# Attention, mixture of experts and feed-forward on one core: shifted low words of the w_in conversion in PSUM, row maxima finished on transposed rows

## The chip, the cores and the metric

The kernel runs on one core of one Trainium2 chip. The metric is the device time in microseconds, the median of several runs. The engines are PE (TensorE, matrix products and transposes), DVE (VectorE), ACT (ScalarE), POOL (GpSimd) and SP (SyncE, which issues the DMAs). Each works through its own queue in order. On chip there are SBUF, and PSUM, into which PE writes and which DVE and ACT can read and write.

## The reference

Three stages follow one another: an attention in which a query sees only keys of its own hash bucket, a soft mixture of eight experts, and h - tanh(h) between two products.

```python
q_bits = (np.einsum('bhsd,dk->bhsk', q, proj) > 0)         # 6 bits; the same for k
mask = q_bucket[:, :, :, None] == k_bucket[:, :, None, :]
scores = np.where(mask, scale * (q @ k.T), -1e9)            # 2 x 8 heads, 768 x 768, 64 wide
scores = scores - np.max(scores, axis=-1, keepdims=True)
attn = np.exp(scores); attn = attn / (attn.sum(-1, keepdims=True) + 1e-09)
x = attn @ v                                                # as 1536 x 512
...
logits = x @ phi                                            # soft experts: softmax over tokens,
slot_input = d.T @ x                                        # over slots, relu(. @ w1[e]) @ w2[e]
...
h = x @ w_in                                                # 512 x 2048, float64
return (h - np.tanh(h)) @ w_out                             # 2048 x 512, float64
```

The weights w_in and w_out arrive as float64. The kernel takes them as pairs of 32-bit words and makes float32 of them with shifts and masks.

## The kernel before, in words

Attention works on eight pairs of heads, numbered i = 0 to 7. For a pair and a chunk of 128 rows there are these pieces of work, each a function that the order strings call by a short name:

- `m` (m_unit, L441): PE makes a 128x768 tile of scores from the leading parts (L446), DVE takes the maximum of each row (L447) into one column of `mx`, 128x12 when the pair is done.
- `f1` (m_fin1, L449): from `mx` DVE makes on 128x12 elements the flag of a row that has no key in its bucket (L454) and its offset (L455), both in `col`.
- `f2` (m_fin2, L458): PE transposes `col` into a PSUM tile `pc` (L462), ACT copies it to `row` (L464), and SP sends the 24 rows of 128 to where they are used: the offsets into row 96 of the operand QA, the flags four times into `z`.
- `s0`, `s1` (s_unit, L500): scores of one head with keys as rows (L504, L506), exponential on ACT (L508), running sum over the keys on POOL (L513, L519). `a` (av_unit, L522): product with v (L531). `xr`, `xe`, `x2`, `x3`, `lg`: row sums (L542), their transposes `prt` (L562) and reciprocals `rs` (L564, L567), tokens by features (px, L587, and xtok, L591), logits (L601, L604).
- `t0`, `t1`, `b`, `h0` to `h3`, `l0` to `l3`, `d`, `kc`, `v1`, `v2`: transposes of q and k (L353), bucket bits (L362, L365), leading parts on ACT (L406), remainders on DVE (L429 to L436), copies, and sums of v (L481 to L497).
- `wl`, `wc` (win_load, win_cvt): w_in comes in 16 parts of 128x512. For each, ACT rescales the high word into `cg` (L174), and DVE runs three instructions: the low word shifted into `cl` (L178), `cg` shifted and joined to it (L187), and the sign bit from the raw high word joined to that, into `win` (L192). `cl` is an SBUF tile of its own.

The order is written out by hand and is the order of every engine's queue:

```python
STEP = ("s0 l1 d s1 a lp m xe s0 m xr e00 v m s1 m s0 l0 m lp m a m s1 l2 v1 m a m m m l3 a wl lp "
        "wc t1 s0 t0 s1 s0 m e01 f1 h0 lp a lp h1 x2 lp wl f2 e02 s1 h3 lp v2 b e03 x3 wc wl s0 s1 "
        "h2 kc a lp wl wc lg qk").split()
```

STEP runs once for each pair i = 0 to 6 ("STEP 2" is the one with i = 2); START goes ahead of it with the first pair's maxima, and LAST serves pair 7. Beside the scores of pair i it finishes the maxima of pair i + 1 and prepares pair i + 2. START converts two of the parts of w_in, STEP 0 to 3 three each, STEP 4 two; STEP 5 and 6 find none left. STEP 5 also holds the first half's weights over its tokens (`e00` to `e03`). `lp` loads pieces of the expert weights, from STEP 5 on, as places come free.

PSUM in attention is a ring of three tiles of 128x768, handed out in turn by `psum()`, and two tiles for the product with v (`pav`). Who asks for the next tile gets the one given out three requests before, and waits until that one's readers are done.

After attention come the experts (the order string MOE) and the feed-forward stage (RUN and a loop), where the words of w_out are converted with the same helper functions in SBUF, and L1184 to L1190 compute h - tanh(h): L1189 reads two SBUF tiles, L1190 an SBUF tile and the PSUM tile `ph`.

Of the kernel before, what the change touches and what calls it, by code (L numbers as in the profile page):

```python
# [10 lines left out]
F32 = mybir.dt.float32  # L11
# [21 lines left out]
# columns of the constant table  # L33
# [8 lines left out]
# from here on, parts that are not on chip all the time  # L42
# [5 lines left out]
# h - tanh(h) = C h z ((z + A)^2 + B), z = h^2, below SMALL  # L48
# [13 lines left out]
# order of the work: before the first pair of heads, for one pair of heads, beside which the next three are prepared, and for  # L62
# the last pair
START = ("const.0 warm.3 qk.0 const.1 tq_aaaa.0 wl.0 oi.0 tk_aavv.0 h1.0 h0.0 bq.0 wl.0 bk.0 h2.0 "
        "h3.0 wq1p.0 m.0 m.0 m.0 l0.0 m.0 const.2 m.0 v.0 wk1a.0 m.0 m.0 m.0 wq0p.0 m.0 kc.0 m.0 "
        "m.0 qk.1 l2.0 m.0 wl.0 d.0 f1.0 wc.0 wk0s.0 t0.1 f2.0 h1.1 t1.1 l1.0 h3.1 l3.0 v1.0 h2.1 "
        "kc.1 oi.1 b.1 v2.0 wc.0 wc.0 h0.1 qk.2 oi.2 wl.0").split()
STEP = ("s0 l1 d s1 a lp m xe s0 m xr e00 v m s1 m s0 l0 m lp m a m s1 l2 v1 m a m m m l3 a wl lp "
        "wc t1 s0 t0 s1 s0 m e01 f1 h0 lp a lp h1 x2 lp wl f2 e02 s1 h3 lp v2 b e03 x3 wc wl s0 s1 "
# [3 lines left out]
# the experts, and the start of the last product with its first chunks  # L73
# [12 lines left out]
def constants():  # L86
# [5 lines left out]
    for pr in range(3):  # L92
        # rows (e2, n2, slot): the slots of expert 2 pr + e2
        ok = ((r % 32)[:, None] == np.arange(32)[None, :]) & (((r % 32) // SPE) == 2 * pr + r // 64)[:, None]
        c[:, C_SELPR + 32 * pr:C_SELPR + 32 * pr + 32] = ok
    for e2 in range(2):
        # rows (n4, slot): the slots of one of the last two experts
        o = C_SELE + 32 * e2
        c[:, o:o + 32] = c[:, C_SEL4:C_SEL4 + 32] * (np.arange(32) // SPE == 6 + e2)
    # mask rows out of bits b: q side [b, 1 - b], k side [-M (1 - b), -M b], for both heads  # L100
    for g in range(4):
        for h in range(2):
            for j in range(2 * NB):
# [7 lines left out]
                if g in (0, 2):  # L111
                    # the first pair of heads: both heads' bits on the q side, the head's own on the k side
                    o = C_FIRST + 2 * (g // 2 + g // 2 * h)
                    c[2 * D // 2 + 2 * NB * h + j, o:o + 2] = m, a
# [11 lines left out]
def body(ctx: ExitStack, tc: tile.TileContext, q, k, v, proj, phi, w1, w2, w_in, w_out, cst, out, dbg=None):  # L126
# [18 lines left out]
    # tokens by features, one half of the batch after the other  # L145
# [24 lines left out]
    # ------------------------------------------------------------------ float64 words to float32  # L170
    # raw [P, n, 2] words (low, high); the exponent is rebased on the high word read as float32
# [27 lines left out]
    # ------------------------------------------------------------------ weights of the experts, in pieces of 8 KB  # L199
    # a piece is half of one expert's w1 (two chunks of 128 rows) or w2 (512 rows, or 256 columns for the last two)  # L200
# [5 lines left out]
    # then places for w_out in halves, and its float64 words, 256 rows at a time  # L206
# [13 lines left out]
    # the first HOLD places take one piece each, and then tiles that stay  # L220
# [28 lines left out]
    # ------------------------------------------------------------------ attention  # L249
    def attention():  # L250
# [6 lines left out]
        # what is done with first comes last  # L257
# [21 lines left out]
        # operands: score products are [kh; mask, 1].[qh; mask, -m] + [kh; kl].[ql; qh]  # L279
        last = NPR - 1  # L280
        # both heads in one tile, but for the places of the last pair
# [21 lines left out]
        mx, cols, zr, vz, es, pav, xtu, rsT, rinv, uses = {}, {}, {}, {}, {}, {}, {}, {}, {}, {}  # L303
# [4 lines left out]
        # the last pair takes places of its weights  # L308
# [22 lines left out]
        # transposes of q or k: rows (head, d), columns (c, p)  # L331
        def t_unit(i, which, engs="aaaa"):
# [3 lines left out]
            if i == 0:  # L336
                # came as (h c d) and not as (c h d): rows (c odd or even, d), columns (half c, p)
# [19 lines left out]
        # bucket bits of q and k, as rows of the mask products  # L357
# [17 lines left out]
        # for the first pair where they go  # L375
# [22 lines left out]
        # leading parts  # L398
# [25 lines left out]
        # remainders, where each of the two inputs sits in the same partitions  # L424
# [14 lines left out]
        # row maxima over the keys, from the leading parts  # L439
# [9 lines left out]
        def m_fin1(i, hs=(0, 1)):  # L449
            n = len(hs)  # L450
            m = mx[i][:, hs[0] * KT:(hs[-1] + 1) * KT]
            col = pre.tile([P, 2 * n, KT], F32, tag="col", name="col")
            zc = col[:, 0:n, :].rearrange("p r c -> p (r c)")
            nc.vector.tensor_scalar(zc, m, -0.5 * MASK, None, ALU.is_lt)  # L454
            nc.vector.scalar_tensor_tensor(col[:, n:2 * n, :].rearrange("p r c -> p (r c)"), zc, -FAR, m, ALU.mult, ALU.subtract)  # L455
            cols[i] = col

        def m_fin2(i, hs=(0, 1)):  # L458
            s, n = i % 3, len(hs)
            col = cols.pop(i)  # L460
            pc = psum("pc")
            nc.tensor.transpose(pc[:2 * n * KT, :P], col.rearrange("p r c -> p (r c)"), ident)  # L462
            row = pre.tile([2 * n * KT, P], F32R, tag="row", name="row")
            nc.scalar.activation(row, pc[:2 * n * KT, :P], AF.Copy)  # L464
            if i not in zr:
                zr[i] = lap.tile([4, KT, P], F32R, tag="z", name="z")
            if QA2[s] is None:
                for j, h in enumerate(hs):
                    copy(QA[s][h][96:97].rearrange("o (c j) -> o c j", c=KT), row[(n + j) * KT:(n + j + 1) * KT, :])
            else:  # L470
                copy(QA2[s][96:97, hs[0]:hs[-1] + 1].rearrange("o h (c j) -> o (h c) j", c=KT), row[n * KT:, :])
            for r in range(4):
                if r % 2 in hs:
                    j = r % 2 - hs[0]
                    copy(zr[i][r:r + 1], row[KT * j:KT * j + KT, :])

        # sums of v over the keys, for rows whose bucket holds no key
# [56 lines left out]
        # row sums, in token layout after x2  # L534
# [35 lines left out]
        # both uses of the sums  # L570
# [24 lines left out]
        # logits of the slots, one head beside the other before the row sums are divided out  # L595
# [18 lines left out]
        # w_in to float32, a part at a time  # L614
# [13 lines left out]
        def win_cvt():  # L628
            if raws:
                raw, c, fq = raws.pop(0)  # L630
                g = cv.tile([P, 512], F32, tag="cg", name="cg")
                l = cv.tile([P, 512], U32, tag="cl", name="cl", bufs=1)
                cvt_b(cvt_a(raw, g, l), win[:, c, fq * 512:(fq + 1) * 512])

        # weights of batch 0 over its tokens, while the other batch goes through attention
        d0 = {}

        def disp0(n):
# [14 lines left out]
            "f1": m_fin1, "f2": m_fin2, "v": load_v, "v1": v_unit, "v2": v_unit2, "qk": load_qk,  # L653
# [7 lines left out]
        for h in range(2):  # L661
            units[f"f1{h}"] = lambda i, h=h: m_fin1(i, (h,))
            units[f"f2{h}"] = lambda i, h=h: m_fin2(i, (h,))
# [49 lines left out]
        # while nothing has arrived yet  # L713
# [57 lines left out]
    # products nobody reads, while the tensor engine would wait and its clock would drop  # L771
# [4 lines left out]
    # weights over the tokens, one half of the batch at a time and with the maxima so far  # L776
# [9 lines left out]
    # the share of the first half has its own maxima  # L786
# [12 lines left out]
    # sums of tokens under those weights, and of the weights: rows (part of the tokens, slot)  # L799
# [20 lines left out]
    # ------------------------------------------------------------------ soft mixture of experts  # L820
# [528 lines left out]
```

## Time and profile before

| | us |
|---|---|
| runs of the kernel before | 533.79, 535.04, 538.79; median 535.04 |
| span of the profiled execution (one execution of its own; the page gives no time beside its span) | 533.6 |
| PE busy, matrix products | 474.6 |
| DVE busy | 388.8 |
| POOL busy | 302.2 |
| ACT busy | 273.3 |

The span is cut in 40 slices in the profile's second part; a digit is the busy share of a slice in tenths, PEclk the clock that was granted to TensorE:

```text
PE   7879787997997879989899899997888888999996
DVE  5959699897998989855814338539999998655552
POOL 4887758676677678757855310006666656444442
PEclk9689799898999999979989999999999999999999
```

The other views are: windows (busy time of each engine in a stretch of the span), groups of instructions by line and shape, one line's instructions with their minimum, median and maximum, timelines of one engine (start, length, and in brackets the idle time before with what ended it), and the chain: the work that ended last, followed back from the end of the span, each step to what released it.

### The profile page before, as it was taken

The page shows a single profiled execution, that of the slowest core. Times are in us where ns is not written, and L with a number is a line of the kernel's source. Part 1 is how long each engine was busy: PE and PEld are TensorE (multiplying, and loading weights), DVE is VectorE, ACT ScalarE, POOL GpSimd, SP SyncE. Part 2 cuts the span into 40 slices and gives each one's busy share as a digit, 9 for nine tenths or more (in the row PEclk, how much of TensorE's full clock was granted, in tenths as well). Part 3 has the DMA queues.
Part 4 walks back from the last instruction along what each step waited for, and adds up shares of the span by engine and source line. Part 5 has one row for each costly group of instructions (what it writes and reads, how often), then busy time and mean ns, then how long its engine had stood idle before and what let it go on. Part 6 is the DMA issues. An engine that isn't in the chain of part 4 may idle for free.

```text
span 533.6 us, 7452 instructions
## 1 busy us (share of the span) xinstructions
PE 474.6 (89%) x2634; PEld 304.8 (57%) x2634; DVE 388.8 (73%) x493; ACT 273.3 (51%) x471; POOL 302.2 (57%) x243
## 2 busy tenths in 40 slices
PE   7879787997997879989899899997888888999996
PEld 3445444555555446555466544365666566888884
DVE  5959699897998989855814338539999998655552
ACT  6344644726546346345244211138767775766662
POOL 4887758676677678757855310006666656444442
PEclk9689799898999999979989999999999999999999
DMA  6445183281631813927538699998000000300003
GB/s 210 107 109 145 48 179 109 65 189 41 143 111 48 202 47 69 327 101 206 220 126 316 266 336 401 364 392 332 1 0 1 1 0 0 119 1 2 1 1 123
DMA packets 51572, 72.83 MB, mean 136 GB/s; under 512 B 25604, under 2 KB 33480, under 8 KB 51528
## 3 DMA queue, kind: packets, MB, share of 16 engines
q1 hardware_dynamic: 51528, 72.28, 42.9%
q8 instruction: 23, 0.38, 0.3%
q14 instruction: 21, 0.17, 0.1%
HBM read 60.08 MB, written 3.15 MB: 118 GB/s over the span
## 4 chain that ended last, share of the span: by engine, by line
DVE 47%; PE 43%; issue 3%; POOL 3%; ACT 2%; DMA 1%; DVEq 0%; SPq 0%; ACTq 0%; POOLq 0%
DVE mx L447 9%; DVE win L192 7%; DVE win L1189 5%; PE pav L531 5%; PE po L1240 5%; PE po L1239 5%; PE po L1241 5%; PE pst L504 4%; DVE win L1190 3%; PE pst L506 3%; DVE KB L429 3%; PE pm L446 3%; DVE win L178 2%; DVE cl L187 2%; DVE col L455 2%
## 5 line engine op out<-in xcount | busy, mean ns | idle before, releaser
L519 POOL TENSOR_TENSOR es<-es,e 128x768 f32<-128x768 f32 x59 | 120.6, 2058 | 44.6 <-ACT e L508 44.5
L508 ACT ACTIVATE e<-pst 128x768 f32<-128x768 f32 x96 | 75.4, 809 | 78.4 <-PE pst L506 77.0
L447 DVE TENSOR_REDUCE mx<-pm 128x1 f32<-128x768 f32 x96 | 87.2, 950 | 15.4 <-PE pm L446 14.2
L531 PE MATMUL pav<-e,tv 128*64 128x256 f32 (+1 forms) x384 | 73.9, 503 | 0.0
L1220 POOL TENSOR_TENSOR split<-win,split 128x512 fp32r<-128x512 f32 x31 | 40.1, 1295 | 53.3 <-ACT split L1215 53.1
L1189 DVE SCALAR_TENSOR_TENSOR win<-win 128x512 f32<-128x512 f32 x64 | 50.6, 791 | 26.6 <-ACT win L1185 26.6
L504 PE MATMUL pst<-QA,KA 128*128 128x512 f32 x192 | 57.2, 381 | 1.5 <-DVE mx L447 0.6
L446 PE MATMUL pm<-KA,QA 96*128 96x512 f32 x192 | 53.1, 380 | 2.3 <-DVE mx L447 1.3
L1220 POOL TENSOR_TENSOR ghl<-win,ghl 128x256 fp32r<-128x256 f32 x32 | 27.7, 865 | 45.5 <-ACT ghl L1215 45.5
L506 PE MATMUL pst<-QB,KB 128*128 128x512 f32 x192 | 51.8, 352 | 0.0
L1239 PE MATMUL po<-w,split 128*128 128x512 f32 x128 | 50.5, 394 | 0.0
L1240 PE MATMUL po<-w,split 128*128 128x512 f32 x128 | 50.4, 394 | 0.0
L1241 PE MATMUL po<-w,split 128*128 128x512 f32 x128 | 50.3, 393 | 0.0
L531 PEld LDWEIGHTS pav<-e,tv 128*64 128x64 f32 x384 | 24.0, 136 | 39.8 <-issue 39.3
L446 PEld LDWEIGHTS pm<-KA,QA 96*128 96x128 f32 x192 | 30.2, 196 | 23.7 <-issue 8.9
L513 POOL TENSOR_TENSOR es<-e 128x768 f32<-128x768 f32 x16 | 29.2, 1828 | 20.8 <-PE pr L542 15.7
L1185 ACT ACTIVATE win<-win,ct 128x512 f32<-128x512 f32 (+1 forms) x64 | 39.5, 617 | 2.1
L1190 DVE SCALAR_TENSOR_TENSOR win<-win,ph 128x512 f32<-128x512 f32 x64 | 35.5, 555 | 6.6 <-DVE win L1189 0.5
L504 PEld LDWEIGHTS pst<-QA,KA 128*128 128x128 f32 x192 | 30.8, 200 | 13.4 <-DVE mx L447 6.4
L1184 ACT ACTIVATE win<-ph 128x512 f32<-128x512 f32 (+1 forms) x64 | 30.6, 478 | 13.2 <-PE ph L1177 13.2
L506 PEld LDWEIGHTS pst<-QB,KB 128*128 128x128 f32 x192 | 31.3, 200 | 4.6
L1177 PE MATMUL ph<-hold,hold 128*128 128x512 f32 x64 | 22.0, 386 | 12.5 <-DVE win L1190 11.9
(244 smaller groups left out, 881.5 us busy)
## 6 DMA issues: line engine op xcount, KB each, us to landing
w<-in_moe_w_dram SPq DMA_DIRECT2D x32, 1024.0 KB
raw<-in_moe_w_in_dram SPq DMA_DIRECT2D x16, 512.0 KB
w<-in_moe_w_out_dram SPq DMA_DIRECT2D x8, 1024.0 KB
tv<-in_v_dram SPq DMA_DIRECT2D x8, 384.0 KB
out_dram<-win SPq DMA_DIRECT2D x12, 256.0 KB
tq<-in_q_dram SPq DMA_DIRECT2D x14, 192.0 KB
tk<-in_k_dram SPq DMA_DIRECT2D x14, 192.0 KB
QB<-QA SPq DMA_DIRECT2D x10, 192.0 KB
```

The lines of the kernel that those rows point to most:

```text
L446: nc.tensor.matmul(pm[:, c0:c1], QA[s][h][:96, c * P:(c + 1) * P], KA[s][h][:96, c0:c1], start=True, stop=True)
L447: nc.vector.reduce_max(mx[i][:, h * KT + c:h * KT + c + 1], pm, axis=AX.X)
L504: nc.tensor.matmul(pst[:, c0:c1], KA[s][h][:, c * P:(c + 1) * P], QA[s][h][:, c0:c1], start=True, stop=False)
L506: nc.tensor.matmul(pst[:, c0:c1], KB[t][h][:, c * P:(c + 1) * P], QB[t][h][:, c0:c1], start=False, stop=True)
L508: nc.scalar.activation(e, pst, AF.Exp, scale=0.125)
L519: eng.tensor_tensor(es[i, h][0], es[i, h][0], e, ALU.add)
L531: nc.tensor.matmul(pav[i][j][64 * h:64 * h + 64, :], tv[i][:, h, c, :], e2[h][:, c0:c1], start=False, stop=c == KT - 1, tile_position=(0, ...
L1189: nc.vector.scalar_tensor_tensor(w, w, Q_B, z, ALU.add, ALU.mult)
L1220: (eng or nc.gpsimd).tensor_tensor(gl[p], g, gh[p].bitcast(F32), ALU.subtract)
L1239: nc.tensor.matmul(po, gh[p][:, us], wo.half(f, 0), start=f == 0, stop=False)
L1240: nc.tensor.matmul(po, gh[p][:, us], wo.half(f, 1), start=False, stop=False)
L1241: nc.tensor.matmul(po, gl[p][:, us], wo.half(f, 0), start=False, stop=f == NF - 1)
```

## The change

Two edits; beside them comments are removed.

First, `win_cvt` takes the place for `cl` from the ring of PSUM tiles instead of from a tile of SBUF. L178 then writes PSUM, L187 reads `cg` in SBUF and `cl` in PSUM and writes PSUM, L192 reads the raw words in SBUF and `cl` in PSUM.

Second, m_fin1 and m_fin2 become one function m_fin at the place of `f2`; `f1` leaves the order strings. PE transposes `mx` itself, 12 rows of 128 in PSUM, and DVE makes flag and offset from there into the rows `zrow` and `row` in SBUF; the copy on ACT goes. The DMAs stay the same in number, size and order, and read from two tiles. Two variants for a single head, which no order string calls, are removed.

```diff
-        "m.0 qk.1 l2.0 m.0 wl.0 d.0 f1.0 wc.0 wk0s.0 t0.1 f2.0 h1.1 t1.1 l1.0 h3.1 l3.0 v1.0 h2.1 "
+        "m.0 qk.1 l2.0 m.0 wl.0 d.0 wc.0 wk0s.0 t0.1 f2.0 h1.1 t1.1 l1.0 h3.1 l3.0 v1.0 h2.1 "
...
-        "wc t1 s0 t0 s1 s0 m e01 f1 h0 lp a lp h1 x2 lp wl f2 e02 s1 h3 lp v2 b e03 x3 wc wl s0 s1 "
+        "wc t1 s0 t0 s1 s0 m e01 h0 lp a lp h1 x2 lp wl f2 e02 s1 h3 lp v2 b e03 x3 wc wl s0 s1 "
...
-        def m_fin1(i, hs=(0, 1)):
-            n = len(hs)
-            m = mx[i][:, hs[0] * KT:(hs[-1] + 1) * KT]
-            col = pre.tile([P, 2 * n, KT], F32, tag="col", name="col")
-            zc = col[:, 0:n, :].rearrange("p r c -> p (r c)")
-            nc.vector.tensor_scalar(zc, m, -0.5 * MASK, None, ALU.is_lt)
-            nc.vector.scalar_tensor_tensor(col[:, n:2 * n, :].rearrange("p r c -> p (r c)"), zc, -FAR, m, ALU.mult, ALU.subtract)
-            cols[i] = col
-
-        def m_fin2(i, hs=(0, 1)):
+        def m_fin(i, hs=(0, 1)):
             s, n = i % 3, len(hs)
-            col = cols.pop(i)
             pc = psum("pc")
-            nc.tensor.transpose(pc[:2 * n * KT, :P], col.rearrange("p r c -> p (r c)"), ident)
-            row = pre.tile([2 * n * KT, P], F32R, tag="row", name="row")
-            nc.scalar.activation(row, pc[:2 * n * KT, :P], AF.Copy)
+            m = pc[:n * KT, :P]
+            nc.tensor.transpose(m, mx[i][:, hs[0] * KT:(hs[-1] + 1) * KT], ident)
+            zrow, row = (pre.tile([n * KT, P], F32R, tag=t, name=t) for t in ("zrow", "row"))
+            nc.vector.tensor_scalar(zrow, m, -0.5 * MASK, None, ALU.is_lt)
+            nc.vector.scalar_tensor_tensor(row, zrow.bitcast(F32), -FAR, m, ALU.mult, ALU.subtract)
...
-                    copy(QA[s][h][96:97].rearrange("o (c j) -> o c j", c=KT), row[(n + j) * KT:(n + j + 1) * KT, :])
+                    copy(QA[s][h][96:97].rearrange("o (c j) -> o c j", c=KT), row[j * KT:(j + 1) * KT, :])
...
-                    copy(zr[i][r:r + 1], row[KT * j:KT * j + KT, :])
+                    copy(zr[i][r:r + 1], zrow[KT * j:KT * j + KT, :])
...
                 g = cv.tile([P, 512], F32, tag="cg", name="cg")
-                l = cv.tile([P, 512], U32, tag="cl", name="cl", bufs=1)
+                l = psum("cl")[:, :512].bitcast(U32)
                 cvt_b(cvt_a(raw, g, l), win[:, c, fq * 512:(fq + 1) * 512])
```

More of the change, by code (lines that the diff above doesn't have):

```diff
@@ L302, in attention @@
         tq, tk, tv, xqs, xks, rowst = {}, {}, {}, {}, {}, {}
-        mx, cols, zr, vz, es, pav, xtu, rsT, rinv, uses = {}, {}, {}, {}, {}, {}, {}, {}, {}, {}
+        mx, zr, vz, es, pav, xtu, rsT, rinv, uses = {}, {}, {}, {}, {}, {}, {}, {}, {}
         def psum(name):
@@ L468, in m_fin2 @@
                 for j, h in enumerate(hs):
-                    copy(QA[s][h][96:97].rearrange("o (c j) -> o c j", c=KT), row[(n + j) * KT:(n + j + 1) * KT, :])
+                    copy(QA[s][h][96:97].rearrange("o (c j) -> o c j", c=KT), row[j * KT:(j + 1) * KT, :])
             else:
-                copy(QA2[s][96:97, hs[0]:hs[-1] + 1].rearrange("o h (c j) -> o (h c) j", c=KT), row[n * KT:, :])
+                copy(QA2[s][96:97, hs[0]:hs[-1] + 1].rearrange("o h (c j) -> o (h c) j", c=KT), row)
             for r in range(4):
@@ L652, in attention @@
             "d": dups, "t0": lambda i: t_unit(i, 0), "t1": lambda i: t_unit(i, 1), "b": bits, "kc": kh1_copy,
-            "f1": m_fin1, "f2": m_fin2, "v": load_v, "v1": v_unit, "v2": v_unit2, "qk": load_qk,
+            "f2": m_fin, "v": load_v, "v1": v_unit, "v2": v_unit2, "qk": load_qk,
             "xr": xr, "xe": xe, "x2": x2, "x3": x3, "lg": logits, "oi": op_init,
@@ L660, in attention @@
             units[f"hp{w}"] = lambda i, w=w: his(i, w, nc.gpsimd)
-        for h in range(2):
-            units[f"f1{h}"] = lambda i, h=h: m_fin1(i, (h,))
-            units[f"f2{h}"] = lambda i, h=h: m_fin2(i, (h,))
         nm = {}
```

## The prediction

> **What bounds the kernel now.** First the page: busy time by engine, and the chain of work that ended last by engine.
>
> ```profile
> PE 474.6 (89%) x2634; PEld 304.8 (57%) x2634; DVE 388.8 (73%) x493; ACT 273.3 (51%) x471; POOL 302.2 (57%) x243
> DVE 47%; PE 43%; issue 3%; POOL 3%; ACT 2%; DMA 1%; DVEq 0%; SPq 0%; ACTq 0%; POOLq 0%
> ```
>
> TensorE is busiest, but VectorE (DVE) holds more of the chain than TensorE does, so which engine limits has to be asked stage by stage. The windows view cuts the span at the ends of the stages (columns: busy time and instructions of PE, PE weight loads, DVE, ACT, POOL; granted clock; DMA share; GB/s).
>
> ```profile
> 40.00:220.00 180.00, 157.92 (x869) 94.38 (x868) 159.12 (x165) 91.85 (x136) 129.17 (x85) 0.96 0.45 112
> ...
> 300.00:370.00 70.00, 64.59 (x587) 35.29 (x586) 42.88 (x75) 20.53 (x48) 10.88 (x21) 0.98 0.97 356
> ```
>
> From 40 to 220 us (STEP 0 to 4, where all but two of the sixteen w_in parts are converted) DVE works 159.1 of 180 us and PE 157.9: two engines that wait for each other. From 300 us on PE is the busier one and the DMA share is 0.97. So I read one step, STEP 2, in the chain (start, us, what).
>
> ```profile
> 119.84 0.96 DVE QB L436
> ...
> 120.82 0.44 DVE cl L178
> ...
> 122.08 2.21 DVE win L192
> ...
> 125.19 0.81 DVE col L454
> ...
> 126.03 1.72 DVE col L455
> ...
> 127.89 0.27 PE pc L462
> ...
> 132.21 0.96 DVE xtok L591
> ...
> 134.39 2.21 DVE win L192
> ...
> 136.62 1.97 DVE cl L178
> ...
> 142.44 0.85 PE pr L542 x8
> ```
>
> Read top down: after the last difference (L436, 119.84) come the three instructions of one conversion (L178, L187, L192), the last row maximum, two tiny instructions on 128x12 (L454, L455) that take 2.5 us together, and only then PE's transpose pc at 127.89. From 132.21 on, behind the xtok product, two more conversions sit on the chain until PE's row sums pr at 142.44. The next view, groups by line and shape, says why (busy us, mean ns; then idle time before).
>
> ```profile
> L192 DVE SCALAR_TENSOR_TENSOR win<-raw,cl 128x512 uint32<-128x512 uint32 x16 | 30.8, 1925 | 0.5
> ...
> L1189 DVE SCALAR_TENSOR_TENSOR win<-win 128x256 f32<-128x256 f32 x32 | 25.4, 793 | 0.0
> ...
> L1190 DVE SCALAR_TENSOR_TENSOR win<-win,ph 128x512 f32<-128x512 f32 x32 | 22.0, 688 | 3.4 <-DVE win L1189 0.5
> ...
> L1190 DVE SCALAR_TENSOR_TENSOR win<-win,ph 128x256 f32<-128x256 f32 x32 | 13.5, 421 | 3.2
> L178 DVE TENSOR_SCALAR cl<-raw 128x512 uint32<-128x512 uint32 x16 | 13.3, 830 | 0.3
> ...
> L493 DVE TENSOR_TENSOR vt<-pv,blk 4x128 f32<-4x128 f32 x8 | 2.2, 279 | 10.7 <-PE pv L489 10.6
> ```
>
> The last instruction of a conversion averages 1925 ns, and above 128x12 took 0.81 and 1.72 us. Length doesn't explain that. L1189 reads two SBUF operands: 793 ns for 256 columns. L1190 reads one of them in PSUM: 421 ns for 256 and 688 for 512, which is work that grows with length. The view of one line alone has L178's minimum, median and maximum:
>
> ```profile
> L178 DVE TENSOR_SCALAR cl<-raw x16: 426/504/1959, 22.0 to 201.9; 128x512 uint32<-128x512 uint32 x16
> ```
>
> And on POOL, at the time of the 2.21 us one:
>
> ```profile
> 133.82 4.46 POOL L519 TENSOR_TENSOR es<-es,e 128x768 f32<-128x768 f32 x2 [0.55 <-ACT e L508]
> ```
>
> POOL's two additions run from 133.82 to 138.28; L192 ends at 136.60 and the following L178 at 138.59, each shortly after an addition could end. I read it so: a DVE instruction with all operands in SBUF may have to wait until POOL's current addition is over, and one that reads PSUM does not.
>
> **The change, part by part.** *Conversion arithmetic.* The same 48 instructions remain; `cl` moves to PSUM. L187 and L192 then have one SBUF and one PSUM input like L1190: 0.69 us each. L178 reads SBUF and writes PSUM, which no row of before does: as an average its bounds are 0.43 (its minimum) and 0.83 us (its mean of before, with the waits for POOL); I take 0.69, the row of the same width that touches PSUM. One conversion is 2.1 us of work, 2.2 with the gaps; the first one of STEP 2 took 3.47 (from 120.82 to 122.08 + 2.21). [...] With 0.43 instead, all places below that wait for a conversion, 14 conversions' worth, would be 0.26 us earlier, 3.6 in all.
>
> *What the conversion now holds.* psum() is one ring of three buffers, so `cl` takes one from PE and hands it on when L192 is done. Two places differ. (A) The first `wc` of STEP stands before t1, s0, t0: t0's third predecessor was a maximum, it is now `cl`. PE's timeline:
>
> ```profile
> 120.70 0.82 PE L353 MATMUL pt<-ct,tq 128*128 128x128 f32 x6
> ...
> 124.64 0.55 PE L562 MATMUL prt<-ct,rsT 128*128 128x128 f32 x3
> ```
>
> Before, t0 started at 120.70. After, the DVE queue ends L436 at 120.80 and the conversion at 123.0, so t0 starts at 123.05: PE stands 2.35 us. From t0 to the end of prt (125.19) there are 4.49 us of PE work, so prt ends at 127.54, with pc right behind it instead of at 127.89: the removed 2.5 us of L454 and L455 pay for the stall, and 0.35 us is left. (B) The other two, behind x3, come before s0, s1, a, lg, s0, s1, a, m. With T = 132.21, xtok ends at T + 0.96, the conversions at T + 3.2 and T + 5.35. PE's second s1 now takes the buffer of the second one:
>
> ```profile
> 137.09 0.53 PE L504 MATMUL pst<-QA,KA 128*128 128x512 f32 x2
> ```
>
> It had started at T + 4.9 and waits 0.45; behind it PE has the rest of s1, a and the maximum m, 2.75 us, until T + 8.1, DVE reduces it until T + 9.1, and pr follows at T + 9.2. Before it was T + 10.23: 1.0 us gained, and there PE is the limit, not DVE. The same stretch, xtok to pr, in STEP 3 and 4 (DVE's timeline, then the chain):
>
> ```profile
> 166.26 0.96 DVE L591 TENSOR_TENSOR xtok<-px,rs 128x768 f32<-128x768 f32 x1 [0.20 <-PE px L587]
> ...
> 201.04 0.96 DVE L591 TENSOR_TENSOR xtok<-px,rs 128x768 f32<-128x768 f32 x1 [0.20 <-PE px L587]
> ```
> ```profile
> 177.22 0.85 PE pr L542 x8
> ...
> 210.01 0.85 PE pr L542 x8
> ```
>
> STEP 3 took 11.0 us, so 1.7 gained; STEP 4, with one conversion left, took 9.0 and loses 0.3, since lg waits for `cl`; STEP 1 has STEP 2's instructions, and I give it the same 1.0. STEP 0 has no x3 or lg; PE had its first maximum ready at 68.5 (timeline), and DVE came to it at 70.33 (chain):
>
> ```profile
> 68.00 0.62 PE L446 MATMUL pm<-KA,QA 96*128 96x512 f32 x2
> ```
> ```profile
> 70.33 0.88 DVE mx L447
> ...
> 71.34 0.85 PE pr L542 x8
> ```
>
> There 1.7 of these 1.8 us are gained. Sum of B: 1.7 + 1.0 + 1.0 + 1.7 - 0.3 = 5.1 us.
>
> *Maxima.* f1 goes (2.5 us of DVE in STEP 2), and ACT's copy (L464). pc now needs only mx. Behind it DVE makes zrow and row, 12x128 out of PSUM, priced as L493 (0.28 each). They queue behind the two rs instructions of x2 and end 1.15 us after pc starts, later than ACT's copy did; the buffer of pc goes to `b`, which loses 0.25 us in the steps that have b and x2. The QA and z copies on SP keep their number and order and start within 0.2 us of before. So A and f together bring 0.1 us in STEP 1 to 4 and 0.4 in STEP 0 (no x2 there): 0.8. In START, f2 stands behind wc and wk0s on DVE, so row is over 2 us later, a conversion's length, and SP sends the mask rows of the next pair behind it: a loss of 0 to 2, I take 1.0; POOL's work covers the rest of START.
>
> STEP 5 and 6 have no conversion, so PE's wait before pc just goes. The windows of what follows pc in STEP 0 to 3, then of the waits before pc in STEP 5 and 6 and of what follows them:
>
> ```profile
> 57.40:62.40 5.00, 5.00 (x20) 3.01 (x21) 1.54 (x3) 3.12 (x6) 2.32 (x2) 0.50 0.13 47
> 92.70:97.50 4.80, 4.80 (x25) 3.28 (x26) 2.00 (x5) 3.45 (x6) 2.71 (x3) 0.64 0.02 3
> 127.90:131.90 4.00, 4.00 (x21) 2.23 (x22) 1.03 (x3) 2.34 (x5) 1.54 (x1) 0.57 0.02 3
> 163.50:167.50 4.00, 4.00 (x29) 2.75 (x29) 2.27 (x5) 3.15 (x6) 1.99 (x2) 1.00 0.03 8
> 228.60:230.90 2.30, 0.00 (x0) 0.00 (x0) 2.25 (x3) 0.01 (x1) 2.16 (x2) 0.93 0.04 14
> 230.90:236.00 5.10, 5.06 (x37) 3.18 (x41) 1.48 (x5) 2.66 (x6) 1.50 (x1) 0.50 0.03 6
> 264.70:267.40 2.70, 0.00 (x0) 0.01 (x1) 2.63 (x4) 0.00 (x0) 2.54 (x2) 1.00 0.40 164
> 267.40:271.60 4.20, 4.18 (x18) 3.19 (x19) 1.46 (x3) 1.39 (x3) 2.06 (x2) 0.59 0.01 2
> ```
>
> PE idles 2.30 us (228.60) and 2.70 (264.70), and behind both the granted clock is 0.50 and 0.59, for 5.1 and 4.2 us. Neither the wait nor the slow stretch remains: 2.4 + 2.0 in STEP 5, 2.7 + 1.5 in STEP 6, 8.6 us together; the 2.0 and 1.5 are about 0.4 of the slow stretch. PE leads the chain from there to the end of attention, so this carries.
>
> *The clock in STEP 0 to 4.* A wait of the same size sits at t0 instead of pc. Behind the waits of STEP 0, 1 and 2 the clock was 0.50, 0.64 and 0.57, behind STEP 3's 1.00. From pc to xtok STEP 2 took 4.32 us and STEP 3 2.76 (163.50, where its window begins, to 166.26), so a drop costs 1.6; for the milder one of STEP 1 I take 1.0. These 4.2 us are given back. After, I give each 2.35 us wait a chance of 0.45: 5 x 0.45 x 1.6 = 3.6. Net 0.6 gained.
>
> *Sum:* 0.8 + 5.1 - 1.0 + 8.6 + 0.6 = 14.1 us, from a span of 533.6 to 519.5. The page has no time around its span; the median of the runs is 1.4 above it (535.04), so I forecast 520.9 us. Own range 513 to 528: the clock -3.6 or +4.4, START 1 either way, L178 at its bounds -3.6 and +2.0.
>
> **The rivals.**
> 1. *Every stall at t0 drops the clock.* Speaking for it: the 228.60 row, 2.30 us idle with 0.50 behind it. Against: 1.00 behind STEP 3's wait. Then the clock term is 4.2 - 8.0: 4.4 us less, 525.3.
> 2. *None of them does.* For it: the stall is shorter than the 2.7 us that STEP 3 passed unharmed. Against: the 228.60 row again. The term is 4.2: 3.6 us more, 517.3. [...]
> 3. *The gain is swallowed later.* From 300 to 370 us the DMA share is 0.97. If expert weights, and not PE, set the end of that stage, the 8.6 us of STEP 5 and 6, which shorten the time in which weights load, are lost: 529.5. Against it: DMA has 1% of the chain, and the loads are issued when PE frees their places, so they move with it.
> 4. *Slower: a conversion in PSUM is longer than I price it.* Place: L178 and L187 write PSUM, which no row prices. If both cost 1.7 us, the conversion grows by 2.0. Each stall at t0 grows by that (5 x 2.0), B by two conversions in STEP 0 to 3 and one in STEP 4 (9 x 2.0): 28 us, 549. It decides from 1.0 us more per conversion on, 3.2 in all, where the 14 us are gone. Against: L1190 shows no penalty for reading PSUM.
> 5. *It doesn't free DVE:* instructions with one SBUF and one PSUM operand still wait for POOL. Then only the maxima's part remains, the 8.6 us less stalls at t0 that are 1.3 us longer each: 533. L1190's 421 ns speaks against it.
>
> **Chances.** Forecast 0.44; rival 1 0.18; rival 2 0.14; rival 3 0.08; rival 4 0.09; rival 5 0.07. A measurement of this kernel can tell about 1% from no change. Faster than 529.7: 0.44 + 0.18 + 0.14 + half of rival 3 = 0.80; within 1%: the other half and rival 5, 0.11; slower than 540.4: 0.09. The range, 511 to 531, takes in rivals 1 to 3 and leaves out 4 and 5.
>
> **What would show it.** Right: L187 and L192 at 0.69 us with hardly a spread; no groups L454, L455 and L464 on the chain; a PE wait of about 2.3 us before pt<-tq in STEP 0 to 4, ended by DVE win; pc directly behind prt; STEP 3 shorter than STEP 2 was; no clock below 0.9 between 228 and 236 us of before. Wrong: conversions above 3 us, PE waiting for `cl` also before s0, s1 or lg for over 1 us, or a stage from 300 to 370 us that is longer by what attention gained.

## The result and the profile after

The changed kernel takes 518.82 us (median of four runs, 517.28 to 519.88), the kernel before 535.20 us beside it (533.79 to 538.79): a ratio of 0.971, 95% interval 0.967 to 0.975. One run of e3 below, 526.6 us at a mean granted clock of 0.959, is left out of its times as slow; the three others, 517.05 to 522.56 us, had 0.975 to 0.981. The forecast was 520.9 us. The profiled execution has a span of 518.0 us, 15.6 less than before; the prediction's sum was 14.1. So the end came out nearly as forecast. The way to it did not, and most of what follows is about that.

The page of the changed kernel: busy time by engine, and the chain by engine.

```profile
PE 474.7 (92%) x2634; PEld 302.3 (58%) x2634; DVE 352.2 (68%) x493; ACT 272.1 (53%) x463; POOL 294.3 (57%) x243
PE 58%; DVE 32%; DMA 3%; SPq 3%; issue 2%; ACT 1%; DVEq 0%; ACTq 0%
```

VectorE is busy 36.6 us less and its share of the chain fell from 47% to 32%. The groups by shape (busy us, mean ns; then idle time before them) answer the prices:

```profile
L187 DVE SCALAR_TENSOR_TENSOR cl<-cg,cl 128x512 uint32<-128x512 uint32 x16 | 11.1, 696 | 6.2 <-ACT cg L174 5.2
L178 DVE TENSOR_SCALAR cl<-raw 128x512 uint32<-128x512 uint32 x16 | 11.0, 688 | 0.2
...
L192 DVE SCALAR_TENSOR_TENSOR win<-raw,cl 128x512 uint32<-128x512 uint32 x16 | 11.0, 687 | 0.5
...
L456 DVE TENSOR_SCALAR zrow<-pc 12x128 fp32r<-12x128 f32 x8 | 2.2, 279 | 0.7 <-PE pc L453 0.7
L457 DVE SCALAR_TENSOR_TENSOR row<-zrow,pc 12x128 fp32r<-12x128 f32 x8 | 2.2, 275 | 0.4 <-DVE zrow L456 0.2
```

All three instructions of a conversion now take 0.69 to 0.70 us, without the spread of before; zrow and row take 0.28. Before, L192 had taken up to 4.4 us (its line, with minimum, median and maximum in ns):

```profile
L192 DVE SCALAR_TENSOR_TENSOR win<-raw,cl x16: 691/2198/4395, 24.1 to 203.3; 128x512 uint32<-128x512 uint32 x16
```

These are the prices of the prediction. What it had no term for stands in the first row of the groups: VectorE idles 5.2 us ahead of L187, for ACT's `cg`.

The windows: STEP 0 to 4, the stage from the end of attention on (it began at 300 us before, at 285 now), then what follows the longest wait of STEP 0, and what follows pc in STEP 5 and 6.

```profile
40.00:220.00 180.00, 163.85 (x907) 96.52 (x907) 134.67 (x170) 94.02 (x135) 128.52 (x90) 0.99 0.46 131
285.00:355.00 70.00, 64.43 (x582) 34.67 (x579) 43.19 (x76) 19.29 (x45) 10.85 (x21) 0.95 0.98 358
54.20:59.20 5.00, 4.96 (x22) 3.80 (x24) 0.88 (x1) 2.85 (x4) 1.51 (x2) 0.69 0.29 105
223.00:228.00 5.00, 4.97 (x71) 3.31 (x71) 2.18 (x9) 3.54 (x7) 4.26 (x4) 1.00 0.03 7
254.00:258.00 4.00, 4.00 (x27) 2.78 (x27) 2.15 (x6) 2.20 (x4) 4.00 (x3) 1.00 0.35 141
```

Behind pc in STEP 5 and 6 the clock is 1.00 where it was 0.50 and 0.59, and PE doesn't wait there. The late stage is as full of DMA as before (0.98) and as full of PE work (64.4 of 70 us).

Where the time came from, by the starts of the same instructions in both timelines (VectorE's first difference of a step, L429, is its mark): the first mark is 1.15 us later; STEP 0 to 4 are 1.18, 1.94, 1.92, 0.97 and 0.32 us shorter, 6.3 together; STEP 5 is 5.24 shorter; from the mark of STEP 6 to the last row sums, 4.4; behind those, 0.7. That sums to 15.5 of 15.6 us.

For the steps with conversions I cut STEP 2 at four places: its mark, pc, the xtok product, the row sums pr, and the next mark (starts in the timelines of VectorE and PE, us). The later columns of this table are the experiments of the next section.

| STEP 2 | before | changed | e1 | e2 | e3 | e4 | e5 | e6 | e7 | e9 |
|---|---|---|---|---|---|---|---|---|---|---|
| mark to pc | 17.58 | 16.57 | 15.02 | 19.08 | 17.33 | 14.72 | 15.35 | 15.78 | 16.54 | 15.49 |
| pc to xtok | 4.32 | 2.97 | 2.77 | 2.77 | 2.96 | 2.77 | 2.84 | 2.96 | 2.96 | 2.83 |
| xtok to pr | 10.23 | 10.66 | 11.32 | 10.65 | 10.06 | 8.78 | 10.07 | 10.66 | 10.06 | 9.18 |
| pr to next mark | 3.47 | 3.48 | 5.02 | 3.50 | 3.47 | 3.48 | 3.48 | 3.47 | 3.49 | 3.47 |
| sum | 35.60 | 33.68 | 34.13 | 36.00 | 33.82 | 29.75 | 31.74 | 32.87 | 33.05 | 30.97 |

Read the first two columns: the gain lies ahead of xtok. From xtok to pr, where the prediction had its largest term of STEP 0 to 4, the changed kernel is 0.4 us *longer* in STEP 2, although VectorE's waits for POOL in that stretch are gone. PE's timeline of that step shows what PE waits for instead (in brackets: idle time, and what ended it):

```profile
119.11 0.88 PE L353 MATMUL pt<-ct,tq 128*128 128x128 f32 x6 [0.20 <-ACT xk L354]
121.15 0.62 PE L497 MATMUL pst<-QA,KA 128*128 128x512 f32 x2 [1.16 <-DVE win L192]
...
124.91 0.27 PE L453 MATMUL pc<-ct,mx 128*12 128x128 f32 x1
...
128.89 0.63 PE L497 MATMUL pst<-QA,KA 128*128 128x512 f32 x2 [0.21 <-DVE xtok L584]
...
134.44 0.62 PE L497 MATMUL pst<-QA,KA 128*128 128x512 f32 x2 [0.90 <-ACT e L501]
...
138.54 0.85 PE L535 MATMUL pr<-es,ones 128*32 128x384 f32 x8
```

VectorE's timeline of the same stretch has the second conversion's gap:

```profile
127.88 0.96 DVE L584 TENSOR_TENSOR xtok<-px,rs 128x768 f32<-128x768 f32 x1 [0.22 <-PE px L580]
...
132.37 0.70 DVE L187 SCALAR_TENSOR_TENSOR cl<-cg,cl 128x512 uint32<-128x512 uint32 x1 [0.80 <-ACT cg L174]
```

t0 (119.11) doesn't wait for the conversion; it waits 0.20 us for the copy of the transposes just ahead of it. The s1 behind it waits for the conversion, 1.16 us. And the second s1 behind xtok (134.44) waits 0.90 us for the exponential of the s0 directly ahead of it. The addresses of the PSUM tiles in the built program say why: contrary to the description of the kernel and to the prediction, the three buffers are not handed out in turn. In STEP 1 (buffer 0, 1 or 2 of each tile, in program order, around the conversions):

```
... pm:2 cl:1 pt:0 pst:2 pt:0 pst:1 pst:2 pm:0 prt:1 pc:2 pst:0 pv:1 pb:2 px:1 cl:0 pst:2 pst:1 cl:2 pl:0 | pst:1 pst:1 pm:2 ...
```

The second `pt` is t0: it gets the buffer that t1 has just had, s1 (the `pst` behind it) gets the one of `cl`, and the first s0 and s1 of the next step the same one, so the second has to wait until the first has been read. STEP 2 to 4 have the same pattern at t0 and s1; in STEP 0 t0 does get the buffer of `cl`, and waits 2.51 us for it.

### The profile page after: what moved, and what is told of

The parts are those of the page before. It is cut to its first block, busy times and chain, and to the rows that moved or that the text cites. A ratio compares the mean times of both kernels' runs of the same rounds, so it can differ in the third digit from the quotient of the medians.

```text
span 518.0 us, 7441 instructions
## 1 busy us (share of the span) xinstructions
PE 474.7 (92%) x2634; PEld 302.3 (58%) x2634; DVE 352.2 (68%) x493; ACT 272.1 (53%) x463; POOL 294.3 (57%) x243
## 4 chain that ended last, share of the span: by engine, by line
PE 58%; DVE 32%; DMA 3%; SPq 3%; issue 2%; ACT 1%; DVEq 0%; ACTq 0%
PE pav L524 9%; DVE mx L447 9%; PE pst L497 6%; PE po L1229 5%; PE po L1230 5%; PE po L1231 5%; PE pst L499 5%; DVE win L1179 4%; PE pm L446 4%; DVE win L192 3%; DVE KB L429 3%; DVE win L1180 3%; DVE win L178 2%; DMA w<-in_moe_w_dram 2%; PE pl L594 2%
## 5 line engine op out<-in xcount | busy, mean ns | idle before, releaser
L512 POOL TENSOR_TENSOR es<-es,e 128x768 f32<-128x768 f32 x59 | 115.9, 1976 | 32.6 <-ACT e L501 32.2
L1229 PE MATMUL po<-w,split 128*128 128x512 f32 x128 | 51.3, 401 | 0.0
L1230 PE MATMUL po<-w,split 128*128 128x512 f32 x128 | 51.1, 399 | 0.0
L1231 PE MATMUL po<-w,split 128*128 128x512 f32 x128 | 50.8, 397 | 0.0
L499 PE MATMUL pst<-QB,KB 128*128 128x512 f32 x192 | 50.4, 344 | 0.0
L1174 ACT ACTIVATE win<-ph 128x512 f32<-128x512 f32 (+1 forms) x64 | 30.7, 479 | 15.5 <-PE ph L1167 15.5
L499 PEld LDWEIGHTS pst<-QB,KB 128*128 128x128 f32 x192 | 30.1, 193 | 4.4
```

What stands on the lines that cost most here:

```text
L499: nc.tensor.matmul(pst[:, c0:c1], KB[t][h][:, c * P:(c + 1) * P], QB[t][h][:, c0:c1], start=False, stop=True)
L512: eng.tensor_tensor(es[i, h][0], es[i, h][0], e, ALU.add)
L1229: nc.tensor.matmul(po, gh[p][:, us], wo.half(f, 0), start=f == 0, stop=False)
L1230: nc.tensor.matmul(po, gh[p][:, us], wo.half(f, 1), start=False, stop=False)
L1231: nc.tensor.matmul(po, gl[p][:, us], wo.half(f, 0), start=False, stop=f == NF - 1)
```

## The experiments

The theory at the start: the two parts of the change pull in opposite directions. The maxima's part brings all of the gain; `cl` in PSUM frees VectorE and costs PE the waits for buffers. The rival: the freed VectorE is the gain.

**e1 and e2: each part alone.**

```diff
# e1: the changed kernel with
-                l = psum("cl")[:, :512].bitcast(U32)
+                l = cv.tile([P, 512], U32, tag="cl", name="cl", bufs=1)
# e2: the kernel before with the opposite line
```

> The changed kernel with cl back in SBUF: the maxima part alone. Theory (the two parts pull in opposite directions; the maxima part is the whole gain): pc stands directly behind prt in STEP 0 to 4 as well, so each of them is 2.7 us shorter than before (13 us in all), the 4.2 us of slow clock behind those waits go, and the 8.6 us of STEP 5 and 6 stay: 535 - 26 = about 509 us, with conversions as long as before (L192 at a mean of 1.9 us). Rival (the conversion in PSUM is the gain, since it takes 24 us off VectorE, and the maxima part brings only STEP 5 and 6): 535 - 9 = 526 us or more.

> The kernel before with cl in PSUM and the maxima worked out as before: the conversion part alone. Theory (opposite signs): the buffer that cl holds makes t0 or t1 wait for the conversion, 1.2 to 2.5 us in each of STEP 0 to 4, and the stretch from xtok to pr is not shorter than before: 535 + 6 to 12 = 541 to 547 us, although VectorE is busy 24 us less. Rival (the conversion in PSUM is the gain): 535 - 8 = 527 us or less.

Measured: e1 520.0 us (516.85 to 523.32; ratio to before 0.971, 0.964 to 0.977), e2 537.4 us (535.38 to 540.82; 1.007, 1.004 to 1.011). So the maxima's part alone is as fast as the whole change, and `cl` in PSUM alone is no gain: the rival falls. Of the theory, the maxima's part is the whole gain; that `cl` in PSUM pulls the other way shows in e2 alone, and weakly, since with the maxima's part it neither costs nor brings anything that the intervals can tell. Both sizes were missed: e2 loses 2.8 us instead of 6 to 12, and e1 stays 11 us short of 509. e1's timeline of PE at the end of that stretch of STEP 1, and the window behind it, show where:

```profile
104.29 0.62 PE L446 MATMUL pm<-KA,QA 96*128 96x512 f32 x2 [1.12 <-DVE lgt L597]
106.10 1.51 PE L535 MATMUL pr<-es,ones 128*32 128x384 f32 x8 [1.20 <-DVE mx L447]
```
```profile
106.00:110.00 4.00, 3.90 (x17) 2.36 (x18) 1.78 (x2) 0.67 (x2) 1.82 (x1) 0.57 1.07 229
```
```profile
L192 DVE SCALAR_TENSOR_TENSOR win<-raw,cl x16: 692/2214/4401, 25.2 to 199.7; 128x512 uint32<-128x512 uint32 x16
```

With `cl` in SBUF, L192 waits for POOL again (the row of one line: minimum, median, maximum), behind xtok up to 4.4 us; lgt and the first maximum are late, PE waits 1.12 and 1.20 us close to each other, and the clock behind that is 0.57: pr to the next mark takes 5.02 us instead of 3.48 in STEP 2, and as much in STEP 1 and 3. In STEP 0 PE waits 4.96 us ahead of pr:

```profile
72.03 1.51 PE L535 MATMUL pr<-es,ones 128*32 128x384 f32 x8 [4.96 <-DVE mx L447]
```

Ahead of pc, though, the same wait costs nearly nothing (15.02 us, against 16.57 with `cl` in PSUM), since PE needs nothing from VectorE there until the last maximum. So a conversion belongs in SBUF ahead of pc and in PSUM behind xtok, and the whole change gives on the one side what it takes on the other.

In e2's STEP 2, where VectorE still has L454 and L455, PE waits twice, for the conversion and again ahead of pc:

```profile
123.93 0.61 PE L504 MATMUL pst<-QA,KA 128*128 128x512 f32 x2 [1.73 <-DVE win L192]
...
129.63 0.27 PE L462 MATMUL pc<-ct,col 128*24 128x128 f32 x1 [1.77 <-DVE rs L564]
```

**e3: the buffers in turn**, as the prediction took them to be.

```diff
+        turn_s = [0]
         def psum(name):
-            return ps.tile([P, S], F32, tag="s", name=name)
+            turn_s[0] += 1
+            return ps.tile([P, S], F32, tag=f"s{turn_s[0] % 3}", name=name, bufs=1)
```

> The changed kernel with its three PSUM buffers handed out strictly in turn, as the prediction took them to be. If the prediction's sum was right in its terms and failed only in the order of the buffers: t0 waits 2.3 us in STEP 1 to 4 (instead of 0.2 and 1.2 us at t0 and s1) and the stretch from xtok to pr in STEP 1 to 3 takes 9.2 us (instead of 10.7): 518.8 + 5 x 1.0 - 3 x 1.4 + up to 5 x 1.6 of clock = 520 to 527 us. Rival (the order of the buffers hardly matters, since VectorE sets the end of that stretch): xtok to pr stays at 10.5 us or more, and the time rises by the longer stall, to 524 us or more even without a lower clock.

Measured: 520.2 us (517.05 to 522.56; 0.970, 0.962 to 0.978), at the lower end of the first expectation, but not by its numbers. The stall at t0 is there, 2.1 to 2.9 us in every step. From xtok to pr it takes 10.06 us, not 9.2. PE's rows of STEP 2 and VectorE's:

```profile
119.49 0.88 PE L356 MATMUL pt<-ct,tq 128*128 128x128 f32 x6 [2.40 <-DVE win L192]
```
```profile
126.83 0.96 DVE L587 TENSOR_TENSOR xtok<-px,rs 128x768 f32<-128x768 f32 x1 [0.22 <-PE px L583]
...
131.32 0.69 DVE L187 SCALAR_TENSOR_TENSOR cl<-cg,cl 128x512 uint32<-128x512 uint32 x1 [0.68 <-ACT cg L174]
```
```profile
132.79 0.62 PE L500 MATMUL pst<-QA,KA 128*128 128x512 f32 x2 [0.30 <-DVE win L192]
...
136.89 0.85 PE L538 MATMUL pr<-es,ones 128*32 128x384 f32 x8
```

The second conversion waits 0.68 us for ACT's `cg`, so it ends at T + 5.9 (131.32 + two instructions of 0.7) instead of T + 5.35, and s1 takes its buffer then, as predicted. From there to pr it is 4.1 us, where the prediction had 3.85. So with the prediction's own ring, its chain of steps holds and its sizes are 0.9 us too good; the order of the buffers is worth another 0.6.

**e4: what VectorE waits for.**

```diff
-                eng.tensor_tensor(es[i, h][0], es[i, h][0], e, ALU.add)
+                if i == NPR - 1:
+                    eng.tensor_tensor(es[i, h][0], es[i, h][0], e, ALU.add)
...
-                                    EPS, None, ALU.add)
+                                    1.0, None, ALU.add)
```

> The kernel before without POOL's additions of the key chunks 2 to 5 to the row sums for the first seven pairs of heads: four of six key chunks are missing from those sums, and 1 instead of 1e-9 is added to every row sum. It shows what VectorE's instructions in SBUF wait for. Theory (they wait for POOL's additions): L192 falls from a mean of 1.93 us to 0.9 or less, L178 from 0.83 to 0.5, L455 from 1.7 us to under 0.3 where POOL is idle. Rival (the instructions are long by themselves, or wait for DMA writes to SBUF): L192 stays above 1.5 us.

Measured: 500.8 us (one run). The lines of e4:

```profile
L178 DVE TENSOR_SCALAR cl<-raw x16: 415/427/1127, 23.6 to 176.6; 128x512 uint32<-128x512 uint32 x16
```
```profile
L192 DVE SCALAR_TENSOR_TENSOR win<-raw,cl x16: 691/693/832, 24.9 to 177.9; 128x512 uint32<-128x512 uint32 x16
```
```profile
40.00:220.00 180.00, 177.10 (x1063) 108.52 (x1062) 142.12 (x189) 107.47 (x161) 51.88 (x51) 1.00 0.57 144
```

L192 falls to 0.69 us with everything in SBUF, and L455 to 0.17 in STEP 2: the waits are POOL's additions. PE is busy 177.1 of 180 us, so this is also what the steps take when PE hardly waits at all: 29.75 us. From xtok to pr in STEP 2 PE was busy 9.03 of 10.23 us before, and is busy all of 8.78 us in e4 (the windows of both):

```profile
132.21:142.44 10.23, 9.03 (x52) 5.69 (x51) 9.92 (x11) 7.00 (x11) 7.15 (x6) 1.00 0.31 89
116.09:124.87 8.78, 8.78 (x52) 5.68 (x50) 6.78 (x10) 7.06 (x12) 2.99 (x4) 1.00 0.09 20
```

VectorE led the chain there, yet in this order of the work no more than 1.5 us could come from freeing it.

**e5 and e6: the first conversion of a step kept away from t0's buffers**, by SBUF and buffers in turn (e5), or by its place alone (e6).

```diff
# e5: on top of e3, "wd" = "wc" with cl in PSUM, "wc" with cl in SBUF
-        "wc t1 s0 t0 s1 s0 m ... e03 x3 wc wl s0 s1 h2 kc a lp wl wc lg qk"
+        "wc t1 s0 t0 s1 s0 m ... e03 x3 wd wl s0 s1 h2 kc a lp wl wd lg qk"
# e6: on top of the changed kernel
-        "wc t1 s0 t0 s1 s0 m ...
+        "t1 s0 t0 wc s1 s0 m ...
```

> The changed kernel with cl in SBUF for the first conversion of a step (the one before t1) and in START, in PSUM for the two behind x3, and with PSUM buffers strictly in turn. Theory (each place of the conversion loses by another thing: in front of t0 by the buffer that cl holds, behind x3 by VectorE's wait for POOL): the stretch from l0 to pc takes 15.0 us in STEP 2, as with the maxima part alone, instead of 16.6; xtok to pr 10.1 us, as with strict turns, instead of 10.7; no wait at t0 in STEP 0 (2.5 us and 1.6 us of clock): 518.8 - 4 x 2.1 - 4 = about 506 to 509 us. Rival (the gain of the one place is lost in the other, since PE only waits elsewhere): 516 us or more.

> The changed kernel with the first conversion of a step put behind t0 instead of ahead of t1 (one word of STEP moved, no other change). Theory (the waits at t0 and at the s1 behind it come from the buffer that cl takes ahead of them, not from VectorE's work): both go, 1.4 us in each of STEP 1 to 4 and 2.5 us and 1.6 us of clock in STEP 0, xtok to pr stays at 10.6 us: about 509 us. Rival (VectorE is late with the last maximum whatever the buffers): pc starts where it did and the time stays within 1% of 518.8 us.

Measured: e5 510.1 us (507.23 to 511.51; ratio to before 0.956, 0.950 to 0.963), e6 512.1 us (511.4 to 513.98; 0.962, 0.956 to 0.968), the kernel before 532.2 us beside both. Both are 1 to 3 us above the theory's numbers; the rivals fall, e6's by the place of pc, which comes 0.8 us earlier in STEP 2, more clearly than by the time. In e5 the first conversion has its wait for POOL back:

```profile
115.97 2.20 DVE L192 SCALAR_TENSOR_TENSOR win<-raw,cl 128x512 uint32<-128x512 uint32 x1
```

and mark to pc takes 15.35 us, 1.2 less than with 0.69 there. In its STEP 0 PE waits 2.18 us ahead of pr, which that theory didn't have. e6 has the same 0.69 us instructions as the changed kernel, and by one word's place its ratio is 0.962 instead of 0.971; its s1 behind t0 waits 0.26 us, for ACT:

```profile
113.90 0.61 PE L497 MATMUL pst<-QA,KA 128*128 128x512 f32 x2 [0.26 <-ACT e L501]
```

So it is the buffer, and not VectorE's time, that cost PE the 1.16 us at s1.

**e7: e6 and the buffers in turn.**

> As the one before, and with the PSUM buffers strictly in turn. Theory: the 0.9 us wait of the second s1 behind xtok for ACT goes too, xtok to pr takes 10.1 us or less in STEP 1 to 3: 1 to 2 us less than the one before, about 507 us. Rival: no difference between the two that the intervals can tell.

Measured: 515.2 us (513.51 to 516.15; 0.966, 0.960 to 0.971), 3 us above e6 where the theory had 1 to 2 us less: it missed, and since the two intervals overlap, its rival is not excluded. xtok to pr is 10.06 us as it said, but in turn `cl` gets the buffer that the last maximum of the stretch ahead of pc takes next:

```profile
119.97 0.62 PE L449 MATMUL pm<-KA,QA 96*128 96x512 f32 x2 [1.03 <-DVE win L192]
```

In STEP 2 that takes back what the turns bring behind xtok (33.05 us in all, against 32.87). Turns are no better in themselves; each order has its own next in line.

**e8 and e10: which instructions wait for POOL.** e8 keeps L178 in SBUF and has only L187 write PSUM; e10 adds one instruction behind each conversion of the changed kernel.

```diff
# e8
+                l = cv.tile([P, 512], U32, tag="cl", name="cl", bufs=1)
+                w, g, l = cvt_a(raw, g, l)
+                o = psum("cl")[:, :512].bitcast(U32)
+                nc.vector.scalar_tensor_tensor(o, g.bitcast(U32), 3, l, ALU.logical_shift_left, ALU.bitwise_or)
+                cvt_b2((w, g, o), win[:, c, fq * 512:(fq + 1) * 512])
# e10
+                nc.vector.scalar_tensor_tensor(l, w[:, :, 1], 0x80000000, g.bitcast(U32), ALU.bitwise_and, ALU.bitwise_or)
```

> The changed kernel with the first word of a conversion (L178) in SBUF again and only the result of its second instruction (L187) in PSUM, so that L187 reads two operands from SBUF and writes PSUM. What makes VectorE wait for POOL? Theory (an instruction waits when all that it reads is in SBUF with two such operands, wherever it writes): the wait moves to L187, whose mean rises from 0.70 to 1.5 us or more, and L192 stays at 0.69. Rival (any operand in PSUM, the output too, takes the instruction out of the wait): L187 stays at 0.70 us without a spread.

Measured: 531.3 us (one run). L187's form is at 0.70 to 0.76 us with one exception (1.52), which looks like the rival. But the wait had only moved ahead of it, to L178 (VectorE, then POOL, in STEP 2):

```profile
135.03 3.51 DVE L178 TENSOR_SCALAR cl<-raw 128x512 uint32<-128x512 uint32 x1
138.65 0.70 DVE L628 SCALAR_TENSOR_TENSOR cl<-cg,cl 128x512 uint32<-128x512 uint32 x1
```
```profile
134.66 3.59 POOL L512 TENSOR_TENSOR es<-es,e 128x768 f32<-128x768 f32 x2
```

L178 begins inside the additions and ends 0.3 us after them; what follows it finds POOL idle. None of the sixteen began inside one of these additions (the exception began inside another of POOL's operations), so e8 leaves the question open, and e10 puts it directly.

> The changed kernel with one more VectorE instruction behind each conversion, 128x512 like the others, that reads two operands from SBUF (the high words and cg), writes cl in PSUM, and whose result nobody reads. In the run before that tried this on L187 none of the instructions began during one of POOL's row sum additions. Here most begin during one. Theory (two operands read from SBUF make it wait for POOL, wherever it writes): a median above 1.5 us. Rival (an output in PSUM takes it out of the wait): 0.70 us without a spread, also where it begins during an addition. In either case the kernel is slower than the changed one, by 0.7 us or more per conversion where VectorE or cl is waited for: 523 us or more.

Measured: 524.8 us (one run). The line of the added instruction, and one of them beside POOL's additions:

```profile
L628 DVE SCALAR_TENSOR_TENSOR cl<-raw,cg x16: 699/1108/2355, 23.5 to 202.0; 128x512 uint32<-128x512 uint32 x16
```
```profile
133.06 0.69 DVE L192 SCALAR_TENSOR_TENSOR win<-raw,cl 128x512 uint32<-128x512 uint32 x1
133.78 1.30 DVE L628 SCALAR_TENSOR_TENSOR cl<-raw,cg 128x512 uint32<-128x512 uint32 x1
```
```profile
132.69 4.06 POOL L512 TENSOR_TENSOR es<-es,e 128x768 f32<-128x768 f32 x2
```

The ten that began inside an addition took 1.09 to 2.35 us, the six others 0.70; two of these six began while POOL filled KA, which reads nothing. The median, 1.11, is below the 1.5 expected because the additions were nearly over, but the split is clean: two operands read from SBUF waited, though the result goes to PSUM. L192 at 133.06, with one of its operands in PSUM, begins inside the same addition and takes 0.69.

**e9: the order behind x3.** On top of e5:

```diff
-        "... e03 x3 wd wl s0 s1 h2 kc a lp wl wd lg qk"
+        "... e03 x3 s0 s1 wd wl h2 kc a lp wl lg wd qk"
```

> As the run with the first conversion in SBUF and strict turns, and with the two conversions behind x3 put where their buffers are free: the first behind s0 and s1 instead of ahead of them, the second behind lg instead of ahead of it. Theory (what is left of the loss behind x3 are waits for buffers: s1 for the xtok product, the second s1 for a conversion that itself waits 0.7 us for ACT's cg): these waits go, xtok to pr falls from 10.1 to 9.0 to 9.3 us in STEP 1 to 3, near the 8.8 us of the kernel without POOL's additions, and the time by 3 to 4 us to 506 to 507 us. Rival (VectorE's own work behind xtok, two conversions and the maximum, sets the start of pr): xtok to pr stays at 10 us and the time within 1.5 us of 510 us.

Measured: 507.05 us (506.18 to 507.55; 0.948, 0.945 to 0.951), within the theory's numbers; it beats both kernels, the changed one by 2.3% (0.948 against 0.971). PE's rows of STEP 2:

```profile
120.96 0.51 PE L500 MATMUL pst<-QA,KA 128*128 128x512 f32 x2
...
125.61 0.51 PE L500 MATMUL pst<-QA,KA 128*128 128x512 f32 x2
...
129.62 0.85 PE L538 MATMUL pr<-es,ones 128*32 128x384 f32 x8
```

Neither s1 waits any more, and xtok (120.44) to pr takes 9.18 us, near the 8.78 of the kernel whose POOL additions are left out. The longest wait of PE that is left lies in STEP 0, 2.44 us ahead of pr.

## Why the prediction was right in its sum and wrong in its parts

The time lies inside the stated range, but not for the reasons given for STEP 0 to 4: there the sum came out by luck. Of the signs that the prediction named, the wait of about 2.3 us before pt<-tq came in STEP 0 alone, and one of the signs of being wrong came too: PE waits for `cl` ahead of s1 for over 1 us (1.16 in STEP 2).

**Right: the reading of VectorE's waits and the prices.** e4 shows that the long conversions waited for POOL; with an operand in PSUM they take the 0.69 us that L1190 had priced. Rivals 4 and 5 fall with that.

**Right: STEP 5 and 6.** 8.6 us predicted, 9.6 measured (5.2 and 4.4). PE's wait before pc and the slow clock behind it are gone. The 2.0 and 1.5 us for the slow clock hold for the profiled execution: such waits don't always lower it (in e2 the wait before pc in STEP 5 was 1.96 us, with a clock of 1.00 behind it, and 2.77 in STEP 6, with 0.57). Rival 3 falls too: from the start of the last row sums (297.2 before, 282.3 after) the span goes on for 235.7 us instead of 236.5, so none of it was given back to the weights' DMA.

**Wrong: the step that failed is B**, "1.7 + 1.0 + 1.0 + 1.7 - 0.3 = 5.1 us", with its premise that "PE's second s1 now takes the buffer of the second one". Measured from xtok to pr: STEP 1 -0.4, STEP 2 -0.4, STEP 3 +0.3, STEP 4 -0.5; from pc to pr in STEP 0, +2.3, part of which is the clock behind pc (0.50 before, 1.00 now). That is 1.3 instead of 5.1. Two errors: psum() is not one ring taken in turn, which costs the 0.9 us wait for the exponential (e3: 0.6 us of the stretch); and the conversions were taken to run without a gap, while the second one waits 0.7 to 0.8 us for ACT's `cg` (e3). The 1.0 us that it asked for in STEP 2 was less than the 1.5 that e4 allows, so the time was there, and e9 gets 1.05 of it (9.18 against 10.23); the changed kernel spends it on these waits.

**Wrong by the premise of buffers in turn, to the good side: A.** It had a stall of 2.35 us at t0 in every step that eats the removed L454 and L455. Measured from L436 to pc: STEP 0 1.1 us longer, STEP 1 to 4 1.0 to 1.4 us shorter, 3.3 together instead of 0.8, since in these four steps t0 waits 0.2 us and s1 1.2. With buffers in turn (e3) the stall of 2.40 is there and pc comes 0.25 us sooner in STEP 2, as the arithmetic for A said (0.35).

**The clock**, 1.00 behind pc in STEP 1 to 4 where STEP 1 and 2 had 0.64 and 0.57, gave 1.7 us from pc to xtok in these steps (+0.9, +1.4, -0.4, -0.2; the losses are of the size of the 0.25 predicted for `b` behind the buffer of pc). With the part in STEP 0 that B's 2.3 holds, this is above the net 0.6, since there was only one wait at t0 of the size expected, STEP 0's of 2.51 us, with a clock of 0.69 behind it. Rivals 1 and 2 supposed five such waits. e3 has them; behind that of STEP 3 the clock was 0.68, behind that of STEP 2 1.00: neither all nor none, and nothing against the chance of 0.45.

So 3.3 + 1.3 + 1.7 = 6.3 us stands against the predicted 0.8 + 5.1 + 0.6 = 6.5: two errors of 2.5 and 3.8 us with opposite signs, and 1.1 us of clock. The premise of buffers in turn is behind the error of A and behind a part of that of B.

**START:** -1.0 predicted, -1.15 measured, but that shows little: the first mark stands at 40.77 us in the changed kernel and at 38.99, 38.93 and 40.48 in e3, e6 and e7, whose START has the same work in the same order. The runs don't separate a loss from that scatter.

## What to carry to other kernels

Time that a busy engine spends waiting on the chain is not all to be had: look at how long the next engine needs for its own work in the same stretch, and take no more than the difference. A tile that moves into a small shared set of buffers costs whoever is next in that set, so read the actual assignment, not the order that one would expect of it, before pricing a wait. The same move can win at one place of a loop and lose at another: here SBUF ahead of pc, PSUM behind xtok, with the conversions put where their buffers are free, were worth more than either everywhere.

## What the runs showed of the hardware

*VectorE and POOL.* An instruction with one operand in SBUF that writes SBUF waited for POOL's additions (L178 in e8 took 3.51 us where it takes 0.43 alone), and so did two operands from SBUF with a PSUM output (e10, up to 2.35 us instead of 0.70) and with an SBUF output (L192 before, up to 4.40 us instead of 0.69). One SBUF operand with the other end in PSUM did not: five L178 of the changed kernel began inside an addition, 0.7 us or more before its end, and took 0.68 or 0.69 us. The price of that was 0.26 us: L178 takes 0.43 us from SBUF to SBUF (its median in e4) and 0.69 from SBUF to PSUM. POOL's additions were longer beside the added instruction, too: the pair behind xtok in STEP 2 takes 4.06 us in e10, where that instruction runs from 1.1 to 2.4 us after the pair's start, and 3.62 at the same place of the changed kernel, which doesn't have it; in e8, where L178 ends 0.3 us after the pair, the pair takes 3.59.

*The clock.* A wait's length alone didn't decide here whether the clock fell. In e3 two waits at t0 were 2.40 us each; behind the one of STEP 3 the clock was 0.68, behind that of STEP 2 1.00:

```profile
153.30:158.30 5.00, 4.98 (x22) 3.83 (x24) 0.83 (x1) 2.81 (x4) 1.53 (x2) 0.68 0.33 105
119.50:124.00 4.50, 4.50 (x29) 3.10 (x30) 0.96 (x1) 3.60 (x5) 2.27 (x3) 1.00 0.37 117
```

In e1 two waits of 1.12 and 1.20 us close together (they end at 104.29 and 106.10) had a clock of 0.57 behind them. In STEP 1 to 4 of the changed kernel s1 waits 1.06 to 1.16 us by itself, and the clock behind each of these waits, over 4.0 to 4.5 us, is 1.00. What decides it stays open here.
